# A written pattern for TensorE's fillers, w_in loaded first, and some sums and scalings on other engines, in a fused cross-attention and PReLU kernel

## The chip, the cores and the metric

The kernel runs on one core of one Trainium2 chip. The metric is the device time of one execution in microseconds (us); before the change it is 213.88 us, the median of three runs.

## What is computed

The inputs are `x` (8 x 8 x 512 x 64: batch, head, token, width), `state` (8 x 8 x 32 x 64), the weights `w_in` (512 x 2048) and `w_out` (2048 x 512), and `alpha` (2048), all float32. Cut to what matters:

```python
scores = scale * x @ state.T                      # per batch and head: 512 x 32
a = softmax(scores);   xread = a @ state          # tokens read the states
a2 = softmax(scale * state @ x.T); sread = a2 @ x # states read the tokens
rows = concat([xread, sread], axis=2)             # 544 rows of 512 per batch, 4352 in all
h = rows @ w_in
g = maximum(h, 0) + alpha * minimum(h, 0)
out = g @ w_out                                   # 4352 x 512, float32
```

## The kernel before

**The stages.** For the token rows, `a @ state @ w_in` is computed as `a @ (state @ w_in)`. So per batch there are four products `m.b.f` (states times a quarter of `w_in`), copied out of PSUM by `mo.b.f`. Then 16 blocks `F.b.jc` of h (128 of the 2048 columns, 512 tokens) from the softmax weights and `m`; `N.b.jc` on ScalarE takes max(-h, 0) and `G.b.jc` on VectorE forms g = h + (1 - alpha) * max(-h, 0). For batch 0 the first four blocks are made in smaller parts (`f`, `n`, `g`), so that they can begin with half of the tokens. The product with `w_out` has two forms. For batches 0 and 1 it is direct: `S.b.q.jc2` adds two of 16 matmuls of a quarter of the tokens, `O` copies the result out and sends it. For batches 2 to 7, and for group 8, the 256 rows that the states read, it is done with seven products `P` of half size in place of eight. They need sums of quarters: `W.i.c` of `w_out`, made once, and `U.b.i.c` of g, per batch; `K` keeps a partial result and `Q` adds, copies out and sends.

**The softmax.** For batch 0 the tokens' scores `tsc.j.g` come from TensorE with tokens on the partitions, one half of the tokens (j) at a time. VectorE takes maxima over each 32 states (`smax`) and subtracts (`ssh.v`), ScalarE takes the exponential (`sexp`), VectorE sums and inverts (`ssum`), GpSimd scales (`snorm.p`), TensorE transposes back (`at`), and `ao` copies out. From batch 1 on the scores `sc.b` come with states on the partitions and are brought over by VectorE's block transposes (`sb`, `wb`), and GpSimd does the subtraction. The states' own softmax uses `tm`, `nb`, `te`, `tsum`, and `tn.b.g`, which scales e2 by the inverse sum on GpSimd; `tt` transposes e2 by DMA, `rd` and `rdo` read the tokens.

**Getting started.** x(0) comes as float32 in two halves on SP's queue (`load_x0`), is cast to float16 by `cx.j.g` and transposed on TensorE (`xt`, copied out by `xo`). The first 256 state rows come on ScalarE's queue; GpSimd casts them (`stc`), TensorE transposes them (`stt`), and `sbd` and `sto` copy them out. All else is loaded by GpSimd's queue, which casts on the way: `wi.f` and `wo.i` (quarters of `w_in` and `w_out`), `lst` (other states), `lx.b` (x of later batches). `xd` transposes later x by DMA from SP's queue.

**The fillers.** `Z.k.n` issues n matmuls of 128x256 on a zeroed tile into PSUM bank k, whose result nobody reads, at places in TensorE's early order.

**The order.** `ORDER` is one list of some 1,100 tokens, each a step with its arguments. The program walks it once, and each engine and each queue gets its instructions in that order; the semaphores are put in from the data. The last letter of many steps names the engine: a ScalarE, v VectorE, p GpSimd. A last number often names the PSUM bank, of which there are six single ones (k0 to k5) and a pair.

Of the kernel before, what the change touches and what calls it, by code (L numbers as in the profile page):

```python
# [8 lines left out]
F32 = mybir.dt.float32  # L9
# [13 lines left out]
f.0.1.0.4 ao.1.a f.0.0.1.2 xt.1.0.0.3 wo.1 mo.2.0.a.1 xo.1.0.1.v mo.1.0.v oma n.0.1.0 g.0.1.0.1 wo.2 n.0.0.1  # L23
xo.1.0.0.v m.1.1 mo.1.1.a m.0.1.1.0 f.0.1.1.3 sc.1 mo.0.1.a.0 mo.0.1.a.1 g.0.0.1.0 g.0.0.1.1 mo.2.0.a.0 f.0.0.0.2
n.0.0.0 tsum.0 tn.0.0 F.0.5.1 n.0.1.1 g.0.1.0.0 S.0.2.1.4 N.0.5 tm.1 F.0.7.0 nb.1.a sb.1 g.0.1.1.1 F.0.6.5 te.1.1
te.1.0 g.0.1.1.0 S.0.1.1.3 tn.0.1 g.0.0.0.0 N.0.6 g.0.0.0.1 smax.1 G.0.6 G.0.5 S.0.1.0 m.0.2 mo.0.2.a N.0.7 S.0.2.0
F.0.4.2 F.0.11.5 N.0.4 G.0.7 G.0.4 N.0.11 G.0.11 S.0.0.1.1 lx.2 wo.3 ssh.p.1 tsum.1 W.1.0.p sexp.1 ssum.1 snorm.p.1
# [5 lines left out]
sc.2 tt.1 sb.2 F.1.11.0 tm.2 rdo.0.a smax.2 F.1.13.2 S.0.0.5 mo.2.2.a.1 S.0.0.7 mo.2.2.a.0 N.1.13 G.1.13 N.1.11
O.0.0.a S.0.3.0.5 G.1.11 nb.2.a te.2.1 S.0.3.7 lx.3 S.0.3.2 F.1.15.3 te.2.0 N.1.15 S.0.3.5 G.1.15 F.1.12.1 F.1.6.2
N.1.12 G.1.12 S.0.3.6 N.1.6 S.0.3.3 G.1.6 S.0.2.7 m.3.3.0.3 mo.3.3.v.1 xd.3 ssh.p.2 sexp.2 ssum.2 mo.3.3.a.0 m.3.2
mo.3.2.a F.1.14.1 W.4.0.p S.1.0.6.2 S.0.3.1 N.1.14 G.1.14 F.1.7.0 O.0.2.a N.1.7 G.1.7 S.1.0.4 F.1.3.3 N.1.3 tsum.2
S.0.3.4 S.1.0.0 m.2.3.4.1 O.0.3.a mo.2.3.v.1 mo.2.3.a.0 m.2.1 mo.2.1.a rd.1.0 m.3.0.5.4 mo.3.0.a.0 S.1.0.3 mo.3.0.a.1
S.1.0.5 sc.3 m.4.0.1.5 mo.4.0.a.0 G.1.3 mo.4.0.a.1 W.3.1.p snorm.p.2 wb.2 lx.4 S.1.3.6.3 F.2.3.4 F.2.2.1 F.2.0.5
S.1.0.7 N.2.3 sb.3 tm.3 G.2.3 rdo.1.a smax.3 N.2.2 G.2.2 N.2.0 S.1.0.1 F.2.8.0 S.1.3.7 W.4.1.p tn.2.1 tn.2.0 ssh.p.3
G.2.0 nb.3.a te.3.0 F.2.1.4 N.2.1 S.1.3.1 te.3.1 tsum.3 G.2.1 S.1.0.2 S.1.3.2 tt.2 N.2.8 G.2.8 O.1.0.a F.2.6.1 N.2.6  # L40
G.2.6 S.1.3.0 F.2.14.5 N.2.14 G.2.14 S.1.1.2.4 F.2.9.2 N.2.9 G.2.9 F.2.10.0 N.2.10 G.2.10 rd.2.1 sexp.3 ssum.3 m.3.1
F.2.5.5 mo.3.1.a F.2.11.2 S.1.3.4 S.1.3.3 S.1.2.1.0 S.1.1.3 N.2.11 G.2.11 rdo.2.a U.2.3.0.p N.2.5 xd.4 G.2.5 S.1.2.5
m.4.1.1.2 mo.4.1.a.1 sc.4 tm.4 S.1.3.5 O.1.3.a tn.3.1 F.2.4.5 tn.3.0 F.2.7.2 mo.4.1.a.0 F.2.13.3 N.2.13 lx.5 sb.4
G.2.13 S.1.1.5 tt.3 F.2.12.1 S.1.1.6 S.1.2.7 F.2.15.3 S.1.2.4 smax.4 S.1.2.3 nb.4.a te.4.0 N.2.4 N.2.7 N.2.12 G.2.4
N.2.15 S.1.2.6 S.1.2.2 S.1.1.0 G.2.7 te.4.1 S.1.2.0 O.1.2.a G.2.15 m.4.3 G.2.12 mo.4.3.a m.5.0.5.2 rd.3.3 rdo.3.a
mo.5.0.v.1 xd.5 m.4.2.1.0 mo.4.2.a.0 snorm.p.3 U.2.1.0.p U.2.2.0.p U.2.4.0.p wb.3 S.1.1.1 S.1.1.7 tsum.4 ssh.p.4
S.1.1.4 F.3.9.2 F.3.7.3 mo.5.0.v.0 sexp.4 lx.6 P.2.1.1.1.1 mo.4.2.v.1 N.3.7 O.1.1.a ssum.4 P.2.1.0.0 N.3.9 G.3.7
# [10 lines left out]
N.4.12 G.4.3 P.3.1.1.0 smax.5 F.4.14.4 K.3.1.a N.4.14 G.4.12 U.3.1.0.p U.3.2.0.p P.3.7.0.1.0 U.3.3.0.p G.4.14
P.3.7.1.1 P.3.6.0.0 F.4.15.1 N.4.15 G.4.15 P.3.6.0.1 P.3.6.1.1 N.4.10 G.4.10 P.3.6.1.0 K.3.2.a F.4.8.5 N.4.8 G.4.8
F.4.13.4 N.4.13 G.4.13 P.3.5.1.1 P.3.5.1.0 P.3.5.0.0 m.5.1 mo.5.1.a m.6.2.1.2 mo.6.2.v.0 m.7.3.5.4 mo.7.3.v.0  # L60
P.3.7.1.0 P.3.7.0.0 sc.6 mo.7.3.a.1 mo.6.2.v.1 sb.6 m.6.1.1.5 rd.4.4 mo.6.1.a.0 rdo.4.a m.7.2.2.1 mo.7.2.a.1 U.3.4.0.p
U.4.3.1.p ssh.p.5 U.4.1.0.p U.4.2.0.p smax.6 P.3.5.0.1 P.4.1.1.0.4 K.3.4.a Q.3.1.1 P.3.2.0.0.1 P.4.1.1.1 sexp.5
# [12 lines left out]
F.6.13.0 G.6.11 P.5.2.0.1 F.6.12.3 smax.7 P.5.7.0.1.1 N.6.12 G.6.12 F.6.8.4 N.6.8 U.5.1.1.p U.5.2.1.p P.5.6.1.1 N.6.13
# [24 lines left out]
def kernel(  # L100
# [675 lines left out]
```

## Time and profile before

| What | Value |
|---|---|
| median of 3 runs (lowest to highest) | 213.88 us (213.56 to 214.23) |
| the profiled execution's own time | 213.49 us |
| its span, first to last instruction | 211.7 us |
| TensorE matmul (PE) | 202.8 us busy, 96% |
| VectorE (DVE) | 173.0 us, 82% |
| ScalarE (ACT) | 144.0 us, 68% |
| GpSimd (POOL) | 182.0 us, 86% |
| mean granted clock of TensorE | 0.997 |
| read and written in HBM | 17.31 MB and 8.91 MB |

All times in the profile are microseconds from the first instruction unless ns is written. PE is TensorE's matmuls, PEld its weight loads, SP the engine that only issues transfers. Matmuls are pipelined: the duration of one is longer than the distance to the next, and a busy PE isn't PE at its peak. In the row of slices each digit is the busy share, in tenths, of one fortieth of the span. A timeline row gives the start, the duration, the engine, the source line, the operation, what is written from what, the shapes, the count, and in brackets the idle time before it with what ended it. The line numbers are those of the kernel before: 220 is the filler, 194, 200, 188 and 157 the loads on GpSimd's queue, 167 and 173 the load and the cast of x(0), 289 `xo`, 363 `smax`, 368 the subtraction, 381 and 382 `ssum`, 385 `snorm`, 436 `tn`, 484 the matmuls of `m`, 508 and 510 `mo`, 533 `F`, 574 and 589 the PReLU, 586 `N`, 603 `S`, 646 `W`, 670 `U`, 691 `P`, 707 `K`, 722 and 724 `Q`.

### The profile page before, as it was taken

The page shows a single profiled execution, that of the slowest core. Times are in us where ns is not written, and L with a number is a line of the kernel's source. Part 1 is how long each engine was busy: PE and PEld are TensorE (multiplying, and loading weights), DVE is VectorE, ACT ScalarE, POOL GpSimd, SP SyncE. Part 2 cuts the span into 40 slices and gives each one's busy share as a digit, 9 for nine tenths or more (in the row PEclk, how much of TensorE's full clock was granted, in tenths as well). Part 3 has the DMA queues.
Part 4 walks back from the last instruction along what each step waited for, and adds up shares of the span by engine and source line. Part 5 has one row for each costly group of instructions (what it writes and reads, how often), then busy time and mean ns, then how long its engine had stood idle before and what let it go on. Part 6 is the DMA issues. An engine that isn't in the chain of part 4 may idle for free.

```text
span 211.7 us, 4977 instructions
## 1 busy us (share of the span) xinstructions
PE 202.8 (96%) x1979; PEld 133.1 (63%) x1979; DVE 173.0 (82%) x259; ACT 144.0 (68%) x280; POOL 182.0 (86%) x119
## 2 busy tenths in 40 slices
PE   4999799999999999999999999999999999999992
PEld 2675334444444445675776887666778668888882
DVE  0598999999999999889998788999799898743141
ACT  2678996789999888868977628796836685520100
POOL 2924689939988999999999899999899998999880
PEclk9999999999999999999999999999999999999998
DMA  5999999478998939403270114991141300022224
GB/s 167 159 193 206 207 196 193 88 136 143 174 144 151 170 82 168 82 3 105 60 185 3 50 62 139 116 247 37 54 99 50 104 0 0 3 96 77 89 86 151
DMA packets 52439, 23.68 MB, mean 112 GB/s; under 512 B 38465, under 2 KB 51393, under 8 KB 52417
## 3 DMA queue, kind: packets, MB, share of 16 engines
q0 software_dynamic: 18816, 8.09, 30.8%
q1 hardware_dynamic: 33328, 15.22, 28.8%
q8 instruction: 15, 0.25, 0.5%
q10 hardware_dynamic: 272, 0.07, 0.1%
q14 instruction: 8, 0.06, 0.1%
HBM read 17.31 MB, written 8.91 MB: 124 GB/s over the span
## 4 chain that ended last, share of the span: by engine, by line
PE 90%; DVE 5%; DMA 2%; issue 0%; ACT 0%; POOL 0%; DVEq 0%
PE h L533 25%; PE px L691 21%; PE o L603 13%; PE pv L691 11%; PE py L691 5%; PE m_ps L484 4%; PE h L542 3%; PE z L220 3%; PE sr_ps L457 2%; DMA st<-in_state_dram 2%; DVE g L574 2%; PE sc L299 1%; PE xT_ps L284 1%; PE st_ps L231 1%; DVE g L589 1%; DVE m L508 1%
## 5 line engine op out<-in xcount | busy, mean ns | idle before, releaser
L589 DVE SCALAR_TENSOR_TENSOR g<-neg,oma_sb,h 128x512 f16<-128x512 f32 (+1 forms) x140 | 92.8, 709 | 8.0 <-ACT neg L586 6.1
L586 ACT ACTIVATE neg<-h 128x512 f32<-128x512 f32 (+1 forms) x140 | 74.6, 579 | 24.7 <-PE h L533 14.7
L533 PE MATMUL h<-aT,m 128*128 128x512 f16 x248 | 66.2, 379 | 0.2 <-DVE g L589 0.2
L691 PEld LDWEIGHTS <-gsum 128*128 128x128 f16 x416 | 40.4, 98 | 9.8 <-issue 0.7
L533 PEld LDWEIGHTS <-m 128*128 128x128 f16 x248 | 23.6, 98 | 20.8 <-issue 1.9
L691 PEld LDWEIGHTS <-g 128*128 128x128 f16 x312 | 30.5, 98 | 7.8
L603 PE MATMUL o<-w_out_sb,g 128*128 128x512 f16 x128 | 33.2, 379 | 1.1 <-DVE g L574 1.1
L670 POOL TENSOR_TENSOR gsum<-g,g 128x1024 f16<-128x1024 f16 (+1 forms) x14 | 27.8, 1988 | 1.6 <-DVE g L589 0.8
L670 POOL TENSOR_TENSOR gsum<-gsum,g 128x1024 f16<-128x1024 f16 (+1 forms) x14 | 27.8, 1988 | 0.9
L670 POOL TENSOR_TENSOR gsum<-g 128x1024 f16<-128x1024 f16 (+1 forms) x14 | 27.8, 1990 | 0.3 <-DVE g L589 0.2
L670 POOL TENSOR_TENSOR gsum<-g,gsum 128x1024 f16<-128x1024 f16 (+1 forms) x14 | 27.7, 1990 | 0.3
L691 PE MATMUL px<-ws,gsum 128*128 128x256 f16 x208 | 27.1, 273 | 0.0
L603 PEld LDWEIGHTS <-g 128*128 128x128 f16 x128 | 11.9, 98 | 16.6 <-issue 1.8
L707 ACT COPY kept<-px 128x512 f32<-128x512 f32 (+1 forms) x15 | 8.4, 561 | 20.2 <-PE px L691 20.2
L385 POOL TENSOR_TENSOR an<-ts,r 128x1024 f16<-128x1024 f32 (+1 forms) x9 | 15.4, 1720 | 5.5 <-DVE r L382 4.0
L368 POOL TENSOR_TENSOR ts<-ts,mx 128x1024 f32<-128x1024 f32 x7 | 13.4, 1911 | 6.9 <-DVE mx L363 6.9
L510 ACT CAST m<-m_ps 128x512 f16<-128x512 f32 x28 | 15.6, 596 | 3.3 <-PE m_ps L484 3.1
L724 DVE TENSOR_TENSOR oq<-pv,kept 128x512 f32<-128x512 f32 (+1 forms) x14 | 9.0, 645 | 10.2 <-PE pv L691 5.7
L691 PE MATMUL pv<-ws,gsum 128*128 128x256 f16 x104 | 15.0, 273 | 0.0
L691 PE MATMUL px<-w_out_sb,g 128*128 128x256 f16 x104 | 14.8, 273 | 0.0
L691 PE MATMUL px<-w_out_sb,gsum 128*128 128x256 f16 x104 | 14.5, 273 | 0.0
L691 PE MATMUL py<-w_out_sb,g 128*128 128x256 f16 x104 | 14.5, 273 | 0.0
(75 smaller groups left out, 268.6 us busy)
## 6 DMA issues: line engine op xcount, KB each, us to landing
out_dram<-oq SPq DMA_DIRECT2D x24, 256.0 KB, 2.2
xg<-in_x_dram POOLq DMA_DIRECT2D x7, 512.0 KB, 7.0
w_in_sb<-in_moe_w_in_dram POOLq DMA_DIRECT2D x4, 512.0 KB, 12.3
w_out_sb<-in_moe_w_out_dram POOLq DMA_DIRECT2D x4, 512.0 KB, 12.5
out_dram<-osb SPq DMA_DIRECT2D x8, 256.0 KB, 3.2
x<-in_x_dram SPq DMA_DIRECT2D x2, 512.0 KB, 5.1
out_dram<-oq SPq DMA_DIRECT2D x4, 128.0 KB, 2.1
st<-in_state_dram POOLq DMA_DIRECT2D x1, 224.0 KB, 5.9
```

The lines of the kernel that those rows point to most:

```text
L368: engine(e).tensor_tensor(blocks(cols(live["ts", b], j, S)), blocks(scored(b, j)), over_blocks(cols(live["mx", b], j, S // N)), ALU.subtract,)
L385: engine(e).tensor_tensor(blocks(cols(live["an", b], j, S)), blocks(cols(live["ts", b], j, S)), over_blocks(cols(live["r1", b], j, S // N) ...
L484: nc.tensor.matmul(t[N * k : N * (k + 1), :], st_head(b, h)[64 * r : 64 * r + 64, :], w_in_sb[64 * r : 64 * r + 64, c, 512 * f : 512 * (f ...
L510: copier(e)(m_tile(b, f)[:, g, :], t[g])
L533: nc.tensor.matmul(h.rearrange("p (r j s) -> p r j s", r=2, j=2), ms[b, f][:, g, 128 * j : 128 * (j + 1)], weights(b, g), start=(g == 0), ...
L586: nc.scalar.activation(neg, h, RELU, bias=0.0, scale=-1.0)
L589: nc.vector.scalar_tensor_tensor(g_tile(b, jc), negs.pop((b, jc)), oma_sb[:, jc : jc + 1], hs.pop((b, jc)), ALU.mult, ALU.add,)
L603: nc.tensor.matmul(outs[b, q], g_tile(b, jc)[:, 128 * q : 128 * (q + 1)], w_out_sb[:, jc, :], start=not begun and jc == 2 * jc2, stop=left ...
L670: engine(e).tensor_tensor(t, x(), y(), op)
L691: nc.tensor.matmul(pbanks[b, name][:, i, :], of(b, c)[:, j, 128 * i : 128 * (i + 1)], moving[:, 4 * c + j, :], start=not begun and j == 0, ...
L707: copier(e)(t, pbanks[b, "x"])
L724: nc.vector.tensor_tensor(osb, pbanks[b, name], kept[b, add], ALU.add)
```

## The change

The fillers multiply a float16 tile that GpSimd writes with `iota` (a different value in each column and partition) ahead of the identity matrix. Sixteen of them are issued before anything else on TensorE, and 16 more stand in the order: 32 in all where there were 51. VectorE no longer clears a zero tile. The cast of the first states can go to VectorE or ScalarE and is given to VectorE, and `wi.0` and `lst` stand first among GpSimd's steps, so that nothing waits ahead of them. `tn` can go to ScalarE, as a multiplication with the inverse sum as scale.

The whole order is another. Counted over it: 17 of 56 `U` and one of 8 `W` are on VectorE and no longer on GpSimd, 7 of 16 `tn` on ScalarE, 49 of 51 `mo` on ScalarE (40 before), three `rdo` on VectorE (none before). On GpSimd the loads are issued in the order wi.0, lst, lx.1, wi.1, wo.0, (`snorm.p.0.0`), wi.2, (`snorm.p.0.1`), wo.1, wi.3, wo.2, wo.3, lx.2; before it was (`stc`), wi.0, lst, lx.1, wi.1, wo.0, wi.2, wi.3, (both `snorm`), wo.1, wo.2, (two `tn`), lx.2, wo.3.

```diff
 ORDER = """
-Z.0.9 cx.0.1.a stc stt.0 sbd.0.v Z.1.5 xt.0.0.1.1 cx.0.0.a xt.0.0.0.2 Z.3.6 sto.v cx.1.0.v sbd.1.a xt.0.1.0.3
-xo.0.0.0.v tsc.0.0.4 xo.0.0.1.a cx.1.1.a tsc.0.1 xt.0.1.1.5 smax.0.0 wi.0 xo.0.1.0.a lst ssh.v.0.0 sc.0.0 xo.0.1.1.a
-tsc.1.0.0 Z.1.2 tsc.1.1 sc.0.1 smax.0.1 ssh.v.0.1 lx.1 wi.1 sexp.0.0 wo.0 wi.2 Z.1.5 m.0.0.1.2 tm.0 wi.3 Z.3.11
-mo.0.0.a.1 ssum.0.0 str.1.3 str.0.5 mo.0.0.a.0 Z.4.13 sexp.0.1 ssum.0.1 snorm.p.0.0 at.0.4 sro.1.v xt.1.1.1.0
-xo.1.1.1.v xt.1.1.0.2 xt.1.0.1.1 snorm.p.0.1 at.1.3 nb.0.a te.0.0 te.0.1 sro.0.a m.1.0 xo.1.1.0.a ao.0.v m.2.0.5.0
+Z.0.2 Z.0.2 Z.0.2 wi.0 lst cx.0.0.a stc.v stt.0 Z.1.2 sbd.0.a cx.1.0.a cx.0.1.v xt.0.0.1.1 xt.0.0.0.2 xo.0.0.0.a Z.3.2
+cx.1.1.v xt.0.1.1.3 xt.0.1.0.4 xo.0.0.1.v sbd.1.v tsc.0.1.5 tsc.0.0 sto.v sc.0.0 xo.0.1.1.a tsc.1.1.1 xo.0.1.0.a
+smax.0.0 ssh.v.0.0 tsc.1.0 smax.0.1 sexp.0.0 ssh.v.0.1 Z.2.2 Z.2.2 lx.1 Z.2.2 m.0.0.2.0 mo.0.0.a.1 sexp.0.1 ssum.0.0
+sc.0.1 tm.0 ssum.0.1 wi.1 mo.0.0.a.0 str.0.3 wo.0 sro.0.a str.1.4 snorm.p.0.0 sro.1.v oma xt.1.1.0.5 xo.1.1.0.v
+xt.1.1.1.0 wi.2 at.0.1 nb.0.a xt.1.0.1.2 te.0.1 xt.1.0.0.3 xo.1.0.0.v te.0.0 ao.0.a m.1.0 mo.1.0.a snorm.p.0.1 at.1.4
...
 """
...
+    pattern = consts.tile([128, 256], F16)
+    nc.gpsimd.iota(
+        pattern, pattern=[[37, 256]], base=-4800, channel_multiplier=29,
+        allow_small_or_imprecise_dtypes=True,
+    )
     ident = consts.tile([128, 128], F16)
     make_identity(nc, ident)
...
-    zero = consts.tile([128, 256], F16)
-    nc.vector.memset(zero, 0.0)
-
-    def zeros(k, n):
-        t = single(k, f"z_{len(zs)}", [128, 256], F32)
+    def fill(k, n):
+        t = single(k, f"fill_{len(zs)}", [128, 256], F32)
         zs.append(t)
         for _ in range(n):
-            nc.tensor.matmul(t, zero[:, :128], zero, start=True, stop=True)
+            nc.tensor.matmul(t, pattern[:, :128], pattern, start=True, stop=True)
 
     zs = []
+    fill(0, 16)
...
-    def first_states_cast():
+    def first_states_cast(e):
         live["st0"] = consts.tile([128, 2, D], F16, name="st0")
-        nc.gpsimd.tensor_copy(live["st0"], st0_32)
+        copier(e)(live["st0"], st0_32)
...
     def token_scores(j, g, k=None):
-        if g == 0:
+        if ("tsc", j) not in live:
...
-    def token_norm(b, g):
+    def token_norm(b, g, e):
         e2 = live["e2", b][:, g, :, :]
-        nc.gpsimd.tensor_scalar(
-            e2, e2, live["r2", b][:, g : g + 1], 1.0, ALU.mult, ALU.mult
-        )
+        r2 = live["r2", b][:, g : g + 1]
+        if e == "a":
+            nc.scalar.mul(e2, e2, r2)
+        else:
+            nc.gpsimd.tensor_scalar(e2, e2, r2, 1.0, ALU.mult, ALU.mult)
...
-        "Z": zeros,
+        "Z": fill,
```

More of the change, by code (lines that the diff above doesn't have):

```diff
@@ L23 @@
[L23 to L27, printed above, removed]
@@ L33 @@
[L33 to L37, printed above, removed]
@@ L38 @@
[L38 to L47, printed above, removed]
@@ L58 @@
[L58 to L62, printed above, removed]
@@ new lines @@
+F.1.9.2 N.1.9 N.1.15 G.1.15 S.0.0.4 m.3.2 S.0.0.0 mo.3.2.a S.0.0.2 S.0.0.1 S.0.0.6 O.0.0.v F.1.11.0 ssh.p.2 sexp.2
+ssum.2 G.1.9 S.1.1.6.5 tn.2.1.a m.2.1 m.3.0.4.1 mo.3.0.a.0 F.1.10.3 N.1.11 S.1.1.2 tn.2.0.p mo.3.0.a.1 N.1.10 G.1.10
+tt.2 S.1.1.0 S.1.0.7.4 S.1.0.3 S.1.0.6 S.1.1.7 mo.2.1.a G.1.11 snorm.p.2 m.2.3.1.2 rd.1.3 wb.2 mo.2.3.a.0 sc.3 sb.3
+mo.2.3.a.1 rd.2.0 rdo.1.a rdo.2.a m.3.3.1.2 mo.3.3.a.0 mo.3.3.a.1 S.1.1.4 lx.4 smax.3 F.2.4.3 N.2.4 tm.3 F.2.10.0
+F.2.15.1 N.2.15 G.2.15 F.2.8.2 N.2.8 G.2.8 N.2.10 S.1.0.4 G.2.4 nb.3.a te.3.1 te.3.0 tsum.3 G.2.10 lx.5 ssh.p.3 sexp.3
@@ new lines @@
+ssh.p.7 F.6.11.4 N.6.11 P.5.6.1.0 U.5.3.0.p F.6.8.0 P.5.6.0.0 G.6.9 G.6.5 N.6.8 G.6.8 tt.7 rd.7.5 rdo.7.v F.6.14.3
+N.6.14 P.5.7.1.1.1 G.6.11 P.5.7.0.1 F.8.7.0 F.6.6.5 P.5.2.0.1.4 G.6.14 P.5.7.0.0 U.5.1.1.p N.8.7 U.5.2.1.v P.5.6.1.1
+N.6.6 P.5.6.0.1 G.8.7 F.8.13.3 F.8.11.0 K.5.2.a P.5.5.1.0 G.6.6 N.8.13 G.8.13 P.5.5.0.1 P.5.2.1.1 F.6.0.5 sexp.7
+ssum.7 F.8.5.3 N.8.5 P.5.5.1.1 G.8.5 N.8.11 N.6.0 P.5.2.1.0 G.8.11 U.5.4.0.p U.5.4.1.p G.6.0 P.5.2.0.0 Q.5.0.0
+snorm.p.7 F.8.4.3 N.8.4 F.6.13.0 P.5.5.0.0 F.8.1.5 G.8.4 U.6.3.1.p wb.7 F.6.15.4 N.8.1 G.8.1 P.5.7.1.0 K.5.4.a Q.5.1.1
```

111 lines of the change are left out of this document (63 added, 48 removed).

## The prediction

> **What bounds the kernel now.** First the page: busy shares and slices.
>
> ```profile
> PE 202.8 (96%) x1979; PEld 133.1 (63%) x1979; DVE 173.0 (82%) x259; ACT 144.0 (68%) x280; POOL 182.0 (86%) x119
> ...
> PE   4999799999999999999999999999999999999992
> ...
> DMA  5999999478998939403270114991141300022224
> ```
>
> TensorE is busy nearly everywhere, but early on that is filler and waiting matmuls. From the trace's matmul starts I charged each real matmul its dense spacing (512 columns 0.216 us, 256 columns 0.109, 128 columns 0.055; eight-tile groups by their dense blocks). That gives about 189.6 us of work in the 211.7 us span. What isn't work stands at 8.4 us by t=9, 13.3 by t=18, 15.4 by t=26, 16.3 by t=32; it grows by only 1.9 us from there to t=207, and the last 4.2 us are the final copies and the write. So only the first 30 us can be shortened, and anything that stalls TensorE later is a loss.
>
> Next the stages (columns: busy us and instructions of PE, PEld, DVE, ACT, POOL; then clock, DMA share, GB/s):
>
> ```profile
> 10.60:15.90 5.30, 5.19 (x86) 3.96 (x85) 5.18 (x9) 4.13 (x11) 1.26 (x3) 1.00 1.54 193
> ...
> 79.00:160.00 81.00, 81.00 (x814) 57.05 (x813) 74.43 (x107) 59.06 (x113) 78.57 (x46) 1.00 0.44 92
> ```
>
> VectorE is full from about t=10 to 30: the softmax chain of batch 0 runs there, and TensorE waits for it. In the middle VectorE has 6.6 us free in 81, GpSimd 2.4. Now the start, from the timeline:
>
> ```profile
> 1.33 2.10 PE L220 MATMUL z<-zero 128*128 128x256 f16 x9 [1.33 <-DVE zero L214]
> ...
> 5.09 0.98 POOL L194 DMA_DIRECT2D w_in_sb<-in_moe_w_in_dram  x1
> ...
> 5.36 1.14 ACT L173 CAST xg<-x 128x512 f16<-128x512 f32 x2 [2.83 <-DMA x<-in_x_dram]
> ...
> 6.61 1.17 POOL L157 DMA_DIRECT2D xg<-in_x_dram  x1
> ...
> 6.87 1.16 DVE L173 CAST xg<-x 128x512 f16<-128x512 f32 x1 [0.73 <-DMA x<-in_x_dram]
> ...
> 7.66 1.47 PE L220 MATMUL z<-zero 128*128 128x256 f16 x6
> ...
> 9.84 0.69 DVE L363 TENSOR_REDUCE mx<-tsc 128x16 f32<-128x512 f32 x1 [1.48 <-PE tsc L337]
> ...
> 19.40 0.48 DVE L574 SCALAR_TENSOR_TENSOR g<-neg,oma_sb,h 128x256 f16<-128x256 f32 x1
> ```
>
> The halves of x(0) land at 5.36 and 6.87. w_in's first block is issued at 5.09, behind GpSimd's cast of the states; its packets begin only at 6.75, just as x(0)'s end. The first `smax` starts at 9.84, the first prelu part at 19.40. These are my two milestones.
>
> **The pattern.** A 256-column filler takes 0.213 us until t=8.7 (nine in 2.10) and 0.109 after 9.2: the clock was at half before. Zeros were multiplied in most of that last stretch and the clock rose all the same, so I give the pattern's values no worth of their own. `iota` is not in the trace; its nearest rows are the 128x128 memset (0.20 us) and affine select (0.29), so 0.2 to 1.0 us for 256 columns; I take 0.5, as it resembles the select at twice the size. Sixteen fillers plus the three pairs ahead of `stt.0` then run from about 1.4: 22 x 0.213 = 4.7, to 6.1, and the clock may rise some us sooner. The Trainium skill (TensorE: Matmul & The Clock Gate, Part 1) says the clock rises after TensorE was busy through a window of about 3.4 us, and that the windows run freely; by it, as an estimate, the rise comes between 4.8 and 8.2. Its price in this kernel: the six fillers at 7.66 held `xt.0.1.0` about 1.0 us (its cast was done at 8.03, its first matmul ran at 9.185). That gain is real only if x(0) is there; otherwise TensorE waits anyway.
>
> **w_in at once.** GpSimd now issues `wi.0` right after `iota` and the identity: 0.73 + 0.5 + 0.6 = about 1.85 instead of 5.09. Packets follow an issue by 1.66 to 1.75 us (5.09 to 6.75; 44.01 to 45.75; 56.00 to 57.75), so at 3.55, while x(0) is on the wire. By the packet records only 543 of its 2048 packets have started then, 34 of 128 per DMA engine. What sharing does is seen from 3.25 to 3.75, where the small state load on ACT's queue overlaps x(0): 166 packets of x(0) against 148 of the states, one for one. A packet of x(0) alone costs an engine 24 ns (170 per 0.25 us on 16 engines), one of w_in 80 (50 per 0.25 us), one of `lst` about 110, of `lx` 23. So the first half of x(0) needs 30 more turns of 24+80: bulk at 6.65, slow engines 0.6 to 0.8 later (as in the landings of before), 7.4 against 5.34. The second half: 2 turns beside w_in (0.2), 8 beside `lst` (1.1), 54 beside `lx.1` (54 x 0.047 = 2.5), bulk 10.5, landing **11.2** against 6.85. Bounds: 6.9 if the queues don't alternate like this, 13.6 if the packets' full durations (27, 98, 170, 41 ns) add up.
>
> After that landing the new order needs: ACT cast 0.62, `xo.0.0.0.a` 0.55 (queued behind that cast of the second half), score matmuls 0.4: `smax.0.0` 1.55 after it, at 12.75 against 9.84: **+2.9**. (VectorE's cast and copies run beside it, 1.25 in all.)
>
> **The chain from there.** VectorE up to the first prelu part: two maxima and shifts 2.6, sum 0.87, `tm.0` 1.13, sum 0.87, `sro.1` 1.02, `oma` 0.12, five PSUM copies 1.8: 8.5 us, against 9.56 in before, where `mo.1.0` (1.23) was on VectorE too. `snorm.p.0.0` comes 1.2 us sooner in it, its sum being ahead of `tm.0`. Added over the orders, VectorE has 25.3 us of rows ahead of TensorE's twentieth us of work against 27.5 before. Gain 1.1 to 2.2, taken **-1.6**. In before w_in's and w_out's blocks land some 2 us ahead of use (third w_in block 23.35, used at 25.55), so loading them sooner brings nothing more; GpSimd's later `wi.2` (behind `snorm.p.0.0`, about 17.3) would land at about 22.6 and `wi.3`, now behind `wo.1` too, at about 27.6 for a use at 28.3 plus the delay: still in time.
>
> **Sums and scalings.** 17 `U` and one `W` go from GpSimd (2.13 us each) to VectorE; 7 `tn` to ACT (0.69 on GpSimd, 0.5 to 0.7 on ACT); nine of 11 `mo` on VectorE go to ACT. VectorE has no row for a sum of two f16 tiles in SBUF: between 0.4 (512-element copies) and 1.24 (1024-element rows); I take 0.7, the row of 512 f32 elements, the same bytes. In the middle (TensorE's work from 62 to 142 us) VectorE's rows add up to 75.8 of 80 against 71.9: seven sums, four more preludes and three `rdo`, less six `mo`. This still fits; ACT rises from 59 to 65.5, also covered. The doubt is the wait: VectorE's cast at 6.87 lasted 1.16 us although ACT's takes 0.62, and ended just after GpSimd's issue at 6.61 (to 7.78): the one seemingly held the other up. If a sum on VectorE waits for GpSimd's running one (busy 0.9 of that stage, 1.06 left on average), 7 x 0.95 = 6.6 us come on top, 2.6 more than the 4.0 free; behind the sum stand preludes, for whose banks TensorE's next `F` waits. No wait 0, all felt 6.6; I take half of the excess, **+1.3**. The Trainium skill (SBUF — State Buffer, Who interferes with whom) states such an exclusive lock for a VectorE instruction with two SBUF inputs against a GpSimd one that reads SBUF; by it the whole 2.6 would come, and no run here has shown that pair yet.
>
> The ten later sums fall where VectorE has 34 us of rows in 48: covered. The tail is the same chain of copy and write: 0.
>
> **Sum** against the profiled execution (213.49 us; span 211.7 and 1.8 around it; 0.39 below the median 213.88): 213.49 + 2.9 - 1.6 + 1.3 = **216.1**.
>
> **Rivals.** *x(0) isn't slowed* (w_in's packets start later than 5.5, because `iota` is slow, or yield to the other queue): landing 6.85, `smax` at 8.4, -1.4 - 1.6 = -3.0, with 0 to 1.3 for the middle: 210.5 to 211.8, faster. It decides at a second landing before 8.6 (with the +1.3) or 9.9 (without). For it: packets of other cases are short, only one overlap was seen; against: that overlap was one for one. Chance 0.29. *Startup lost, middle hidden*: VectorE's sums don't wait: 213.49 + 1.3 = 214.8. For it: 6.6 us free in the middle of before. Chance 0.14. *Both in full*: second half at 13.6, +5.3 - 1.1 + 2.6: 220.3. Chance 0.15. *The pattern does nothing that zeros didn't*: likely so, and inside every case at no cost.
>
> **Numbers.** Forecast 0.42, its own range 214.5 to 218.5. The range goes from the first rival with the whole gain (-1.4 - 2.2: 209.9) to the third: 209.8 to 220.5. A measurement of this kernel can tell about 0.3%, 0.64 us. Faster 0.29 (first rival, nearly all), same 0.05 (0.04 of the second, a little of the first), slower 0.66.
>
> **What would show it.** Right: w_in's first packets at 3 to 4 us; ACT's cast of x(0)'s second half waiting for DMA until 10 or later; first `smax` near 12.7 and first prelu part near 21; sums on VectorE longer than 0.7 us when GpSimd runs one, TensorE gaps behind them. Wrong: the second half landing before 9, `smax` before 10, or TensorE's non-work at t=32 below 15 us. Least sure is how two queues share an engine; a different answer there moves the time by 4 us.

## The result, and the profile after

The changed kernel takes **222.38 us** (median of 4 runs, 220.69 to 231.58) against 213.72 us for the kernel before, run beside it: **1.0386 times** as long, 95% interval 1.0292 to 1.0479. One of the four runs (231.58) was disturbed, at a lower clock, and is not in the ratio. The forecast was 216.1 us, in a range of 209.8 to 220.5: the direction was right, the size was not. The profiled execution took 220.69 us, 7.2 more than the one of before (213.49), with a span of 218.5 instead of 211.7.

The table gives TensorE's time that isn't work (as in the prediction: the elapsed time less the dense spacing of the real matmuls so far) at equal points of the work, from the matmul starts of the traces.

| useful work done, us | before | after |
|---|---|---|
| 10 | 15.1 | 12.8 |
| 20 | 16.2 | 13.9 |
| 60 | 17.3 | 15.2 |
| 70 | 17.4 | 18.4 |
| 100 | 17.9 | 21.4 |
| 140 | 18.0 | 24.0 |
| 189 (end) | 18.1 | 24.9 |

So the start, where I had forecast a loss, **gained** 2.4 us (16.3 to 13.9 at t=32), and from there on the kernel lost 11.0 us where before lost 1.8: a difference of 9.2. The net of 6.8 is the difference of the spans.

The page after, with busy times, TensorE's slices and the chain of work that ended last, and then the chain's line of before:

```profile
PE 202.1 (92%) x1960; PEld 130.5 (60%) x1960; DVE 187.3 (86%) x275; ACT 149.5 (68%) x289; POOL 144.9 (66%) x94
...
PE   7868999999999994989998999899989999999992
...
PE 64%; DVE 21%; DMA 6%; ACT 6%; issue 2%; POOL 1%; POOLq 0%; DVEq 0%; SPq 0%
PE h L539 17%; PE px L697 15%; PE o L609 10%; DVE g L595 8%; PE pv L697 8%; DVE gsum L676 5%; DMA e2T<-e 4%; PE py L697 4%; PE fill L223 3%; PE h L548 3%; PE m_ps L490 3%; DMA xT<-xg 2%; ACT neg L592 2%; PE sr_ps L463 2%; DVE nb L409 2%; DVE ts L334 2%
```

```profile
PE 90%; DVE 5%; DMA 2%; issue 0%; ACT 0%; POOL 0%; DVEq 0%
```

TensorE's busy sum is nearly what it was (202.8), but between t=80 and 164 its slices now have a 4 (82 to 87 us) and four 8s, where before they were all 9. In the chain VectorE has 21% instead of 5%, of it the sums (`gsum`, L676) 5% and the prelu parts (`g`, L595) 8%; the DMA that transposes the scores (`e2T`) has 4%. The middle stage (columns as in the prediction):

```profile
79.00:160.00 81.00, 74.67 (x793) 51.17 (x790) 77.64 (x103) 60.33 (x115) 65.02 (x35) 1.00 0.48 92
```

GpSimd went from 78.6 to 65.0 us, as meant; VectorE from 74.4 to 77.6, with 3.4 us free; TensorE from 81.0 to 74.7. The engine that stands still is not full, and neither is the one that it waits for.

The start, from the timeline of after:

```profile
0.84 0.34 POOL L184 IOTA pattern<- 128x256 f16 x1 [0.40 <-POOLq L766]
...
1.24 5.31 PE L223 MATMUL fill<-pattern 128*128 128x256 f16 x22 [1.24 <-POOL pattern L184]
...
1.64 0.97 POOL L199 DMA_DIRECT2D w_in_sb<-in_moe_w_in_dram  x1
...
5.05 0.78 POOL L205 DMA_DIRECT2D w_out_sb<-in_moe_w_out_dram  x1
5.46 0.62 ACT L173 CAST xg<-x 128x512 f16<-128x512 f32 x1 [2.91 <-DMA x<-in_x_dram]
5.46 0.62 DVE L173 CAST xg<-x 128x512 f16<-128x512 f32 x1 [0.29 <-DMA x<-in_x_dram]
...
6.97 0.43 DVE L173 CAST xg<-x 128x512 f16<-128x512 f32 x1 [0.89 <-DMA x<-in_x_dram]
...
9.14 0.69 DVE L367 TENSOR_REDUCE mx<-tsc 128x16 f32<-128x512 f32 x1 [0.26 <-PE tsc L341]
...
17.91 2.44 DVE L580 SCALAR_TENSOR_TENSOR g<-neg,oma_sb,h 128x256 f16<-128x256 f32 x6 [0.16 <-ACT neg L576]
```

w_in is issued at 1.64, but the casts of x(0)'s halves start at 5.46 and 6.97, only 0.10 us later than before; first `smax` at 9.14 (9.84 before), first prelu part at 17.91 (19.40).

The middle, at the first sums on VectorE:

```profile
80.47 1.90 POOL L372 TENSOR_TENSOR ts<-ts,mx 128x1024 f32<-128x1024 f32 x1
...
80.94 1.99 DVE L676 TENSOR_TENSOR gsum<-g,g 128x1024 f16<-128x1024 f16 x1
...
82.34 2.56 POOL L676 TENSOR_TENSOR gsum<-g 128x1024 f16<-128x1024 f16 x1
...
82.96 2.49 DVE L676 TENSOR_TENSOR gsum<-gsum,g 128x1024 f16<-128x1024 f16 x1
...
85.37 2.71 DVE L595 SCALAR_TENSOR_TENSOR g<-neg,oma_sb,h 128x512 f16<-128x512 f32 x4
...
86.16 0.59 PE L539 MATMUL h<-aT,m 128*128 128x512 f16 x2 [2.77 <-DVE g L595]
```

A sum that starts while GpSimd runs ends 0.55 us after GpSimd's instruction: 82.37 to 82.92, 84.90 to 85.45, and so, within 0.03 us, for eight more, which last 0.67 to 2.33 us. Beside an idle GpSimd it takes 0.68 us, so two of the eight (0.67 and 0.68 us, begun close to GpSimd's end) were not held up. GpSimd's next instruction, which starts in the sum's shadow, is stretched as well, 2.56 instead of 2.13. Four prelu parts stand in VectorE's queue behind the two sums, TensorE's next `h` needs their banks, and TensorE stands for 2.77 us. After t=30 TensorE has eight gaps with 8.3 us in all above one matmul's spacing (before has none of this size): 5.0 behind such sums (at 83, 114, 118 and 159 us), 2.2 ahead of the state reads at 97.7 and 141.5, and 1.0 ahead of two other groups. The state reads wait for the transposed scores:

```profile
97.72 0.68 PE L463 MATMUL sr_ps<-e2T,xg 128*64 128x32 f16 x32 [1.08 <-DMA e2T<-e]
```

The new order issues four of the eight transpositions only 3.4 to 4.8 us ahead of their use: 51.90 for 55.71, 92.89 for 97.72, 138.09 for 141.46 and 151.94 for 155.72. In before the same four had 4.6, 16.8, 4.4 and 3.3 us. The one at 92.89 also took 4.7 us to land, where in before the eight took 3.0 to 4.1.

### The profile page after: what moved, and what is told of

Its sections match the earlier page's. It is cut to its first block, busy times and chain, and to the rows that moved or that the text cites. A ratio compares the mean times of both kernels' runs of the same rounds, so it can differ in the third digit from the quotient of the medians.

```text
span 218.5 us, 4936 instructions
## 1 busy us (share of the span) xinstructions
PE 202.1 (92%) x1960; PEld 130.5 (60%) x1960; DVE 187.3 (86%) x275; ACT 149.5 (68%) x289; POOL 144.9 (66%) x94
## 4 chain that ended last, share of the span: by engine, by line
PE 64%; DVE 21%; DMA 6%; ACT 6%; issue 2%; POOL 1%; POOLq 0%; DVEq 0%; SPq 0%
PE h L539 17%; PE px L697 15%; PE o L609 10%; DVE g L595 8%; PE pv L697 8%; DVE gsum L676 5%; DMA e2T<-e 4%; PE py L697 4%; PE fill L223 3%; PE h L548 3%; PE m_ps L490 3%; DMA xT<-xg 2%; ACT neg L592 2%; PE sr_ps L463 2%; DVE nb L409 2%; DVE ts L334 2%
## 5 line engine op out<-in xcount | busy, mean ns | idle before, releaser
L595 DVE SCALAR_TENSOR_TENSOR g<-neg,oma_sb,h 128x512 f16<-128x512 f32 (+1 forms) x140 | 93.0, 704 | 9.7 <-ACT neg L592 9.1
L539 PE MATMUL h<-aT,m 128*128 128x512 f16 x248 | 66.9, 379 | 3.9 <-DVE g L595 3.9
L676 POOL TENSOR_TENSOR gsum<-g,g 128x1024 f16<-128x1024 f16 (+1 forms) x11 | 22.4, 2035 | 19.0 <-PE px L697 12.5
L697 PE MATMUL px<-ws,gsum 128*128 128x256 f16 x208 | 28.1, 273 | 0.9 <-DVE gsum L676 0.9
L676 POOL TENSOR_TENSOR gsum<-g 128x1024 f16<-128x1024 f16 (+1 forms) x12 | 25.0, 2086 | 2.5 <-DVE g L595 1.3
L516 ACT CAST m<-m_ps 128x512 f16<-128x512 f32 x36 | 19.8, 598 | 4.4 <-PE m_ps L490 4.1
L676 POOL TENSOR_TENSOR gsum<-g,gsum 128x1024 f16<-128x1024 f16 (+1 forms) x9 | 18.9, 2098 | 2.3 <-DVE gsum L676 1.3
L372 POOL TENSOR_TENSOR ts<-ts,mx 128x1024 f32<-128x1024 f32 x7 | 13.4, 1910 | 6.4 <-DVE mx L367 6.4
L713 ACT COPY kept<-px 128x512 f32<-128x512 f32 (+1 forms) x16 | 9.2, 576 | 8.3 <-PE px L697 8.3
L676 POOL TENSOR_TENSOR gsum<-gsum,g 128x1024 f16<-128x1024 f16 (+1 forms) x7 | 14.0, 2003 | 1.2 <-DVE gsum L676 0.8
L697 PE MATMUL pv<-ws,g 128*128 128x256 f16 x104 | 13.8, 273 | 0.0
```

The lines of the kernel that those rows point to most:

```text
L372: engine(e).tensor_tensor(blocks(cols(live["ts", b], j, S)), blocks(scored(b, j)), over_blocks(cols(live["mx", b], j, S // N)), ALU.subtract,)
L516: copier(e)(m_tile(b, f)[:, g, :], t[g])
L539: nc.tensor.matmul(h.rearrange("p (r j s) -> p r j s", r=2, j=2), ms[b, f][:, g, 128 * j : 128 * (j + 1)], weights(b, g), start=(g == 0), ...
L595: nc.vector.scalar_tensor_tensor(g_tile(b, jc), negs.pop((b, jc)), oma_sb[:, jc : jc + 1], hs.pop((b, jc)), ALU.mult, ALU.add,)
L676: engine(e).tensor_tensor(t, x(), y(), op)
L697: nc.tensor.matmul(pbanks[b, name][:, i, :], of(b, c)[:, j, 128 * i : 128 * (i + 1)], moving[:, 4 * c + j, :], start=not begun and j == 0, ...
```

## The experiments

Theories for the middle: *lock* (VectorE's two-input sums and GpSimd exclude each other), *load* (VectorE simply has too much to do), *order* (the new order itself is late somewhere, whatever the sums take). Ratios are to the kernel before, run beside each.

**Sums back to GpSimd.** The changed kernel, all 18 sums on GpSimd again, order kept:

```
-W.3.1.v ... U.2.1.1.v U.2.2.1.v ... U.8.4.1.v
+W.3.1.p ... U.2.1.1.p U.2.2.1.p ... U.8.4.1.p
```

> The changed kernel with its 18 sums given back to GpSimd, at the same places of the order. Theory A (lock: a sum of two SBUF tiles on VectorE waits for the operation that GpSimd is running; in the trace after, the sums at 80.94 and 82.96 took 1.99 and 2.49 us and ended about 0.55 us after GpSimd's operations did, and TensorE then stood still 2.8 us): TensorE's non-work between t=60 and 190, 10.0 us after and 1.3 before, falls to 3 or less, and the time to 212 to 215. Theory B (load: VectorE merely has some 12 us more to do): the same fall; the second batch of runs tells A from B. Theory C (the rest of the new order, with copies and scalings on ScalarE and later DMA transposes, costs it): the time stays at 219 to 222. If GpSimd's 38 us more become the bound of an order that was made without them: 215 to 218.

Measured 225.34 us (1.0524, 1.0472 to 1.0575), above all that was expected. With the seven scalings back on GpSimd as well (`tn.*.a` to `tn.*.p`):

> The changed kernel with the 18 sums and the seven scalings given back to GpSimd. If the scalings on ScalarE (0.73 us each) cost something of their own, this is faster than the run with the sums alone by over 0.6 us; if GpSimd is the bound without them, slower by 1 to 3; theory A and B say nothing of them: within 0.6.

Measured 238.72 us (1.1016, 1.0939 to 1.1094), 13.4 us above the run before it and not 1 to 3. The gap at 83 us is still there, now for GpSimd's sum. In the first of the two runs:

```profile
86.61 0.61 PE L697 MATMUL px<-ws,gsum 128*128 128x256 f16 x4 [2.89 <-POOL gsum L676]
```

In the second TensorE stands there from 83.85 to 90.52, again for a sum on GpSimd. This order has its sums early because they are shared out, and in these two runs GpSimd alone doesn't deliver them in time. Undoing a part inside the new order therefore measures another lateness and doesn't price the lock.

**The same sums in the old order.** The kernel before, with the same 18 sums on VectorE (`U.2.1.1.p` to `U.2.1.1.v`, and so on):

> The kernel before with the same 18 sums on VectorE, and nothing else of the change. Theory A: some 7 of them fall in the full stage, stretched to 1.5 to 2.5 us: +3 to +9, 217 to 222. Theory B: each costs 0.7 us where VectorE has 6.6 us free in the middle: +0 to +3, 214 to 217. Theory C: within 0.5 of 213.7.

Measured 234.49 us (1.0975, 1.0949 to 1.1002), far above even the lock theory's 222. One weight sum alone holds VectorE for 4.34 us, through GpSimd's DMA issue, its following sum and a scaling, and TensorE stands 3.69 us:

```profile
55.59 1.21 POOL L157 DMA_DIRECT2D xg<-in_x_dram  x1 [0.72 <-PE sr_ps L457]
55.82 4.34 DVE L646 TENSOR_TENSOR ws<-w_out_sb 128x1024 f16<-128x1024 f16 x1
...
56.82 2.13 POOL L646 TENSOR_TENSOR ws<-w_out_sb,ws 128x1024 f16<-128x1024 f16 x1
...
61.38 1.89 PE L533 MATMUL h<-aT,m 128*128 128x512 f16 x4 [3.69 <-DVE aT L393]
```

Behind that gap 512-column matmuls stood 0.43 us apart instead of 0.216: the granted clock was at half from 59.5 to 66.3 us. So the run shows the lock's reach, but its price here includes the slower clock.

**Two inputs against one.** The kernel before, with one more short VectorE instruction behind each of the 17 `U` that the change moves (the expectations say 16):

```
 U.2.1.1.p
+D            # nc.vector.tensor_tensor(st_pairs, w_out_sb[:, 0, :], w_out_sb[:, 1, :], subtract)
              # or, in the second run: nc.vector.transpose(st_pairs[:, :256], w_out_sb[:, 0, :256])
```

> The kernel before, with one more VectorE instruction behind each of 16 of the GpSimd sums that the change moves (the same places in the order): a subtraction of two 512-element f16 tiles in SBUF, written to a tile that nobody reads any more. It adds 16 times about 0.4 us of work to VectorE and changes nothing else. Lock theory (a VectorE instruction with two SBUF inputs and a GpSimd one that reads SBUF exclude each other): most of the 16 last 1.0 to 2.5 us, and GpSimd's sums beside them 2.3 to 2.6 instead of 2.13; the additions cost VectorE some 15 to 25 us and the time is 219 to 232 us. Load theory (only VectorE's added work counts): all 16 last 0.4 to 0.5, time 213.5 to 215.

> As the run with 16 added two-input instructions, but each of the 16 has one input: a VectorE transpose of 256 f16 columns, about as long alone (0.43 us by estimate). Lock theory: all 16 last 0.4 to 0.5 us whatever GpSimd does, time 213.5 to 215. Load theory: the same time as with the two-input instructions, within 1 us.

Measured 232.00 us (1.0871, 1.0823 to 1.0918) with two inputs, 215.67 us (1.0109, 1.0088 to 1.0130) with one. The groups by shape (busy us and mean ns of one), first with two inputs and then with one:

```profile
L730 DVE TENSOR_TENSOR st_pairs<-w_out_sb 128x512 f16<-128x512 f16 x17 | 24.8, 1457 | 0.2
```

```profile
L730 DVE STREAM_TRANSPOSE st_pairs<-w_out_sb 128x256 f16<-128x256 f16 x17 | 7.5, 440 | 0.2
```

The first pair with two inputs in the timeline, each held to the end of a GpSimd instruction (86.71 and 88.97) and 0.28 to 0.29 us beyond:

```profile
84.80 1.91 POOL L386 TENSOR_TENSOR an<-ts,r 128x1024 f16<-128x1024 f32 x1
...
85.15 4.10 DVE L730 TENSOR_TENSOR st_pairs<-w_out_sb 128x512 f16<-128x512 f16 x2
...
86.67 2.30 POOL L671 TENSOR_TENSOR gsum<-g,gsum 128x1024 f16<-128x1024 f16 x1
```

Alone they last 0.42 and 0.44 us. With one input they last that beside any GpSimd instruction; with two the mean is 1.46 and the time 16.3 us longer. Seventeen more instructions as such cost 2.4 us (I had expected 0.2 to 1.7); the lock, and the half clock that followed two of its gaps (granted 0.5 from 88.9 to 95.7 and from 184.4 to 191.3 us), cost the rest. The Trainium skill (SBUF — State Buffer, Who interferes with whom) states that a VectorE instruction with two SBUF inputs contends with a GpSimd instruction that reads SBUF, as an exclusive lock, and one with at most one SBUF input outside the two-port modes does not; both halves agree with these two runs. The number of inputs alone doesn't tell, though. VectorE's cast of x(0) from f32 to f16 (L173) reads one tile and takes 0.43 us alone (6.97 in the changed kernel). In seven of the traces it began 0.24 to 0.55 us into a DMA issue on GpSimd, and each time it ended 0.25 us after that issue: 1.16 us at 6.87 in before, 0.62 at 5.46 after. In seven others it began at most 0.22 us into one and took its 0.43. So the one row on which the prediction had based its doubt was read rightly.

**What the lock costs in the changed kernel.** First, the 17 `gsum` sums on VectorE replaced by one-input transposes of the same bytes (the addition is left out), order kept:

```
-engine(e).tensor_tensor(t, x(), y(), op)
+nc.vector.transpose(t as f32, one of the inputs as f32)     # on VectorE only
```

> The changed kernel with its order as it is, but each of the 17 gsum sums on VectorE is replaced by a one-input VectorE transpose of the same 2 KB per partition (the addition is left out); by estimate 0.55 to 0.75 us each, near the 0.68 that a sum takes beside an idle GpSimd. Lock theory: they last that long throughout, TensorE doesn't stand at 83 to 86 us, and the non-work at the end of the work falls from 24.9 us to 16 to 19: time 212 to 215. Order theory (the new order itself is late there): 217 to 221 although they are short. Load theory: the same 217 to 221.

Measured 222.10 us (1.0420, 1.0377 to 1.0463): the instructions last 0.70 us, the stalls behind sums are gone, and the time is no better. The state reads now wait longer, and the granted clock is at half behind the first two gaps, from 58.0 to 61.4 and from 99.0 to 105.8 us (the expectation of the next run says some 2 us):

```profile
57.80 0.93 PE L463 MATMUL sr_ps<-e2T,xg 128*64 128x32 f16 x32 [1.84 <-DVE ts L334]
...
100.30 1.04 PE L463 MATMUL sr_ps<-e2T,xg 128*64 128x32 f16 x32 [3.32 <-DMA e2T<-e]
```

The first row names VectorE, whose instruction ended at 57.69; but the transposed scores had landed only at 57.67, so either can have held this read.

Then the same, with four state reads and their copies 8 to 24 steps later in the order, and the changed kernel, sums and all, with only these reads later:

```
-... rd.1.3 ... rd.2.0 rdo.1.a rdo.2.a ... S.1.1.4 lx.4
+... rd.1.3 ... rdo.1.a ... S.1.1.4 rd.2.0 rdo.2.a lx.4      # rd.4, rd.5, rd.6 likewise
```

> The run with one-input transposes in place of VectorE's 17 sums, and in addition four state reads of the order (rd.2, rd.4, rd.5, rd.6 with their copies) 8 to 24 steps later, so that the transposed scores (e2T), which come by DMA, have 2 to 5 us more before TensorE needs them. The profile of that run had gaps of 2.1, 3.7 and 0.9 us in front of just these reads, and half a clock for some 2 us behind the first two. If the new order loses by the lock and by these late DMAs together: both gone, non-work at the end 16 to 18 us instead of 26.5, time 212 to 215. If something else in the order holds TensorE: 217 or more.

> The changed kernel, whole, with the same four state reads later and nothing else. Lock and late DMA together: the reads' gaps (1.2 and 1.0 us in the profile of the changed kernel, 2 to 6 in other executions) go, the gaps behind the sums (2.8, 0.4, 0.8, 1.0) stay: 217 to 220, 2 to 3 us faster than the changed kernel's median. Lock alone: no change, 220.5 to 223.

Measured 214.97 us (1.0053, 1.0025 to 1.0081) and 221.98 us (1.0412, 1.0349 to 1.0476). The medians together:

| | sums with two inputs | one-input instructions |
|---|---|---|
| reads where the change puts them | 222.38 | 222.10 |
| reads 8 to 24 steps later | 221.98 | 214.97 |

The same place in the two runs of the lower row:

```profile
83.62 2.49 DVE L676 TENSOR_TENSOR gsum<-gsum,g 128x1024 f16<-128x1024 f16 x1
86.03 2.05 DVE L595 SCALAR_TENSOR_TENSOR g<-neg,oma_sb,h 128x512 f16<-128x512 f32 x3
...
86.82 1.01 PE L539 MATMUL h<-aT,m 128*128 128x512 f16 x2 [3.13 <-DVE g L595]
```

```profile
81.51 0.71 DVE L678 STREAM_TRANSPOSE gsum<-gsum 128x512 f32<-128x512 f32 x1
...
83.03 3.57 DVE L595 SCALAR_TENSOR_TENSOR g<-neg,oma_sb,h 128x512 f16<-128x512 f32 x5 [0.18 <-ACT neg L592]
83.06 0.59 PE L539 MATMUL h<-aT,m 128*128 128x512 f16 x2
```

Either limit alone holds the kernel at 222; with both lifted 7 us come back. None of the seven sums between 79 and 160 us had waited for its inputs in the changed kernel (VectorE was idle ahead of them for 0.04 us at most), so the input that the transposes leave out isn't what was gained. The expectation from both theories together held for the run without two-input sums (212 to 215); for the one with them the lock alone was enough, against the 217 to 220 I had put there. In its trace the gap at 83 us is followed by half a clock (86.1 to 89.5 us), which the changed kernel's was not, and one gap of 0.9 us ahead of a read stays (56.98). The one kept trace of the changed kernel doesn't show the gaps of 2 to 6 us that this expectation names for other executions. Lock and late transposed scores are each a limit that the other hides. Why the transposed scores took up to 7 us from issue to use without the lock (93.23 to 100.30), against 4.8 with it, beside an x load issued in both 0.3 us later, was not separated.

**The start alone.** The kernel before, in its own order and on its own engines, with only the pattern, the 16 fillers, w_in and the second state load first on GpSimd, and the states' cast on VectorE:

```
-Z.0.9 cx.0.1.a stc stt.0 ... smax.0.0 wi.0 xo.0.1.0.a lst ssh.v.0.0
+wi.0 lst cx.0.1.a stc.v stt.0 ... smax.0.0 xo.0.1.0.a ssh.v.0.0      # fill(0, 16) ahead of all
```

> The kernel before with the change's start alone: pattern by iota, sixteen fillers first in place of nine, first states cast on VectorE, w_in's first block and the states issued first. The rest of the order as before. In the trace after, TensorE's non-work at t=32 is 13.9 us against 16.3: if that comes from these edits and the middle keeps it, 211 to 212; if it comes from the new order of batch 0's softmax, within 0.6 of 213.7; if the middle gives it back (VectorE or GpSimd being the bound there), 213 too, with the non-work at t=32 lower all the same.

Measured **212.08 us (0.9923, 0.9901 to 0.9945)**: 0.8% faster than the kernel before, with the interval clear of 1. Which of the edits brought it was not separated. First `smax` is at 8.27, and its non-work (14.6 us at 20 us of work) stays 1.2 to 1.6 below that of before to the end. The same with a tile of zeros:

```
-nc.gpsimd.iota(pattern, ...)
+nc.gpsimd.memset(pattern, 0.0)
```

> The order of before with the start's edits (the run that took 212.1 us), but the pattern tile is set to zero by a memset instead of iota: fillers, order and loads unchanged. Theory N (the values multiplied don't matter; my forecast): the clock doubles at 5.4 us as with the pattern, first smax at 8.3, time within 0.3 us of the pattern's, 212 to 212.5. Theory P (the pattern is what brings the clock up): it doubles at 8 to 9 us, the transposes and scores of x(0) between take twice as long, first smax 0.5 to 1 us later and time 212.7 to 213.5.

Measured 212.13 us (0.9919, 0.9895 to 0.9943). The written values do nothing: five fillers take 0.72 us at 5.5 with the pattern and 0.72 at 5.3 with zeros, where before six took 1.47 at 7.7. What goes with the earlier rise is that TensorE is kept busy from 1.2 to 4.8 us, by whatever values: in the fifteen traces that begin so the granted clock rose at 4.2 to 7.0 us, in the four that begin as before at 8.3 to 10.4. The Trainium skill (TensorE: Matmul & The Clock Gate, Part 1) goes by time busy and not by the number of instructions, and its window of some 3.4 us, running freely, gave 4.8 to 8.2 for the rise as an estimate; the rises at 5.4 and (in the changed kernel) 6.1 lie in it, and eight more of the fifteen. The other five came at 4.2 to 4.6, down to 2.9 us behind the first filler, so the estimate's lower end is too high by these measurements.

**Why w_in didn't slow x(0).** Three runs in the order just shown: the second state load moved later, a GpSimd instruction that waits for x(0)'s cast put behind w_in's load, and five more `iota` ahead of it:

```
-wi.0 lst cx.0.1.a ...
+wi.0 cx.0.1.a ... xo.0.1.0.a lst      # first run
+wi.0 cx.0.1.a D lst                   # second: D = nc.gpsimd.tensor_scalar(wait_tile, xg part, 1.0, 1.0, mult, mult)
+D wi.0 lst cx.0.1.a                   # third: D = five iota
```

> The order of before with the start's edits (pattern, w_in first), except that the second state load goes back behind x(0)'s last copy, and with it, behind it on GpSimd, the loads of x(1), w_in and w_out: w_in's first block is GpSimd's only DMA issue in the first 8 us. Theory Y (w_in's packets wait until x(0)'s are through): first packets again at about 5.6 us, x(0)'s halves at 5.1 to 5.5 and 6.6 to 7.0, time 211.5 to 213. Theory B (the packets are released when GpSimd has got through its run of issues, at 5.8 in the changed kernel): first packets at 3.0 to 3.6, packets of x(0) and w_in then alternate one for one as I had forecast, x(0)'s second half lands at 8 to 11, first smax at 10 or later, time 213 to 216.

> The order of before with the start's edits; behind w_in's first load GpSimd runs a small multiplication of a part of x(0)'s cast first half, so that its next loads are issued only after 5.5 us and w_in's is the only one before. Theory Y (w_in's packets wait until x(0)'s are through) and theory L (they follow the issue by 4 us): first packets at 5.4 to 5.8 us. Theory B (they are released at the end of GpSimd's run of issues): at 2.6 to 3.6, and x(0)'s second half lands after 8.

> The order of before with the start's edits; five more iota of 256 columns ahead of the first, so that w_in's first load is issued some 1.4 to 1.7 us later, at 3.1 to 3.4 us. Theory Y (yield to x(0)): first packets still at 5.4 to 5.8. Theory L (4 us behind the issue): 7.0 to 7.5. Theory B (end of the run of issues, then at about 7.3): 7.2 to 7.6.

Measured 212.49 us (0.9962, 0.9947 to 0.9976), 212.11 and 212.91 (one run each). The first run missed its aim: nothing on GpSimd waits between the two loads, so they were issued at the same times as without the edit. From the packet records:

| | w_in issued | its first packet | x(0)'s last packet started | x(0)'s packets left at w_in's first, of 2048 |
|---|---|---|---|---|
| before | 5.09 | 6.78 | 6.49 | 0 |
| after | 1.64 | 5.52 | 6.57 | 251 |
| w_in alone on GpSimd | 1.65 | 5.72 | 6.27 | 154 |
| w_in later | 3.60 | 6.39 | 6.37 | 0 |

With GpSimd idle behind the issue (its next instruction came at 5.87) the packets began no sooner, so they don't wait for a run of issues. Nor do they follow the issue by a constant: 1.7, 3.9, 4.1 and 2.8 us. In all of them they begin as x(0) runs out. Plain yielding foretold 5.4 to 5.8 for the last row, though, and it was 6.39, so the rule is not settled. The Trainium skill (DMA: Bandwidth & Descriptors, Queues, rings and completion order) states a round robin between queues per packet; the traces show it where both have packets on the wire (in after, alpha's against w_in's own: 98 to 97 from 7.25 to 7.75; against x(1)'s: 326 to 326 from 11.0 to 11.5), but it doesn't tell when the software queue's first packet comes, and that decided here.

**Is the start's gain separate?** The first 112, 157 and 182 steps of the changed kernel, then the remaining steps in the order and on the engines of before (`tn.*` on GpSimd, no `U` on VectorE); the 157 in two forms:

> The changed kernel's first 112 steps (up to the negative part N.0.6, TensorE's first 25 to 30 us), then all remaining steps in the order and on the engines of before: the new start without the sums and scalings moved. If start and middle are separate: the start's gain of 2.4 us (16.3 to 13.9 us of non-work at t=32) is kept to the end, 210.5 to 212. If the new start is bought with steps that come due later (its loss in the middle belongs to it): 214 or more.

> The changed kernel's first 157 steps (to about t=35 us, with names of two of batch 0's output quarters and of two PSUM banks exchanged so that the rest fits on), then all remaining steps in the order and on the engines of before. The seam is later than in the run with 112 steps, where TensorE had lost its cover at 21 to 26 us. If the start's gain is separate from the middle: non-work 13.6 to 14.2 us at t=32 and 1.9 more to the end, time 210.3 to 212. If the start is bought with later steps: 214 or more.

> The changed kernel's first 157 steps as they are, then the remaining steps in the order and on the engines of before (there two of batch 0's output quarters and two PSUM banks are exchanged so that it fits on). Separate parts: non-work 13.6 to 14.2 us at t=32 and at most 2 more by the end, time 210 to 211.5. Start bought with later steps: a gap of over 1 us after the seam and 212.5 or more.

> As the run with the changed kernel's first 157 steps, but with the first 182 (to the negative part N.0.15, all of batch 0's and 1's scalings on their new engines among them, none of the sums on VectorE). If the 2.0 us were the seam's: no gap over 1 us behind t=25, non-work 13.6 to 14.4 at t=32 and 15.5 to 16.3 at the end, time 210.5 to 211.8. If the start itself is paid for later: gaps of together 1.5 to 2.5 us come again after the new seam (35 to 45 us), time 212.2 or more.

Measured 216.77 (1.0157, 1.0133 to 1.0182), 214.00 (1.0041, 1.0019 to 1.0064), 212.46 (0.9942, 0.9920 to 0.9963) and 212.89 us (0.9974, 0.9953 to 0.9996). The first two took TensorE's cover away at 21 to 26 us, where gaps of 2.2 us came, and say nothing on the question. The last two keep the start as it is and lose 1.7 to 2.0 us in gaps between 31 and 48 us, behind either seam. Their non-work at the end is 16.8 and 17.5 us against 18.1 in before, so of the 2.4 us only 0.6 to 1.3 is separate. The 0.7 us between the two stands already at 10 us of work, where the clock had risen at 4.2 us in the one and at 6.4 in the other. What the rest bought, probably work on batch 1 done early, was not isolated.

## Why the prediction was right or wrong

The start came out 3.7 us better than the sum had it (+1.3 forecast, 2.4 gained), the middle 7.9 us worse (+1.3 forecast, 9.2 lost). Both have a step that failed; the one in the middle made the time too long.

- **w_in's packets slow x(0): +2.9.** Wrong, and the step is "packets follow an issue by 1.66 to 1.75 us, so at 3.55". They came at 5.52, so x(0)'s second half was cast at 6.97 and not at 11.2. The delay is no constant. The first of the three rows that it was read from (5.09) was itself issued while x(0) was on the wire, and its packets came 0.29 us behind x(0)'s last, so that row couldn't tell a fixed delay from a wait for x(0). The packets given at 45.75 and 57.75 started at 45.95 and 57.91, so the three delays were 1.70, 1.94 and 1.91 us. In the changed kernel a load on GpSimd's queue shows 1.93 us with nothing else on the wire (55.74), and 2.61 and 3.70 where other queues moved over 0.5 MB meanwhile (100.81 and 93.21). The one-for-one sharing itself was real. (A packet of `lst` costs 133 ns by the count that gave the others, 30 per 0.25 us, and not 110; that is 0.2 us on eight.) My rival "packets start later than 5.5, or yield" described what happened, and its -3.0 for the start is near the 2.4 gained; I gave it 0.29.
- **Shorter chain on VectorE: -1.6.** About right in sum, and less than forecast on the milestones: from `smax` to the first prelu part it took 8.77 us instead of 9.56, a gain of 0.8 where I had 1.1 to 2.2. Of the start's 2.4 us, 0.7 came ahead of the first `smax` and 1.7 behind it; the splices kept 0.6 to 1.3 of the 2.4.
- **`iota` 0.5, fillers to 6.1, w_in issued at 1.85, nothing gained by the pattern's values:** measured 0.34, 6.55, 1.64, and 212.13 with zeros against 212.08.
- **A sum at 0.7:** 0.68 beside an idle GpSimd.
- **The wait: +1.3.** Right mechanism, mis-sized term. I put 6.6 us on VectorE if every sum waits; the seven sums between 79 and 160 us took 11.9 us instead of 4.8, 7.1 more. Then I let 4.0 us of VectorE's free time absorb it and halved the rest. That is the step that failed. VectorE still had 3.4 us free in that stage, but the prelu parts that stood behind the sums came late all the same, and TensorE stood for 5.0 us behind them. The price by the pair of runs, with the state reads later in both, was 7.0 us. The rule of the Trainium skill (SBUF — State Buffer, Who interferes with whom), which I had put at 2.6, was right as a rule; the 2.6 was my arithmetic of free time.
- **Not in the sum at all:** the new order's state reads, some 3.4 to 4.8 us behind their DMA's issue. I compared loads and sums of engines per stage and never the distance between each DMA's issue and its use.
- **Later sums covered, tail 0, ScalarE covered:** nearly right. The first of the ten, at 174.49, waited too (1.60 us), and TensorE stood for 0.56 us at 178; from 140 us of work to the end the non-work grows by 0.9 us, against 0.1 in before.

The rival that named the time best ("both in full", 220.3) came near it by luck. It had the wrong start in it, and its two errors had opposite signs: +5.3 for a start that gained, and +2.6 for a middle that lost 9.2.

## What to carry to other kernels

Before moving work from GpSimd to VectorE, count the SBUF inputs of the instruction: with two, each one that started beside a GpSimd instruction here lasted beyond that instruction's end (once beyond the end of three in a row), so price the instructions queued behind it, not VectorE's free time. One input is no safe sign by itself: the f32 to f16 cast of x(0) was held up by GpSimd's DMA issues. Where a new order is planned, compare for each DMA the distance from issue to use with the old one; two limits can hide behind each other, and then only the pair of edits shows either. Of this change the part worth keeping is the smallest, the start's edits together: w_in first and TensorE kept busy from the start (212.08 us), with zeros as well as with a pattern.

## What the runs showed that I had not expected

- A VectorE instruction with two SBUF inputs that starts beside a GpSimd one ended 0.55 us after it (1024 f16 columns; 0.68 alone), and stretched the GpSimd instruction that started meanwhile from 2.13 to 2.56 us. A GpSimd DMA issue held one as well: the weight sum at 55.82 in the old order, which alone would have ended at 56.50, was still waiting when the issue ended at 56.80.
- GpSimd's `iota` of 128x256 took 0.34 us.
- Behind gaps of 2.1 to 6.7 us the granted clock fell to half for 3.4 or 6.8 us in eight of these traces (full matmuls 0.43 us apart instead of 0.216), so a stall is paid for a second time. It isn't the gap's length alone: the 3.05 us gap at 83 us in the changed kernel, and one of 3.27 us at the same place with the sums back on GpSimd, were followed by no such stretch, one of 3.40 us in the run with the reads later was.
